# GpSimd in place of VectorE for 31 small softmax reciprocals, and later slots for work that waits on small DMAs

## The chip, the cores and the metric

The kernel runs on one core of a Trainium2 chip. The metric is the device time of one launch in microseconds (us), the median of several runs. Profiles are of one execution each; their span runs from the first to the last instruction, and times inside them count from the span's start.

## The reference

```
xn  = layernorm(x)                                    # x: 1 x 2048 x 512, bf16
q,k,v = split(xn @ wqkv)                              # 32 heads of 16
p   = softmax(q k^T * 16**-0.5)                       # 32 heads, 2048 x 2048 each
att = (p v, heads side by side) @ wo
g   = xn @ W_gate;  u = xn @ W_up                     # 512 -> 1792
out = x + att + (max(g, 0) * u) @ W_down
```

## The kernel before

One core does an attention block and a gated block of the same input. Queries are cut into four column blocks of 512 (`c4`), heads into four groups of eight (`gg`), each of which is done in two halves of four heads (`ee`). That makes 32 blocks `(c4, gg, ee)`, numbered n = 0 to 31. A block goes over 16 key tiles of 128 (`kt`), with four heads side by side: TensorE (PE) makes the scores (L1018), their exponential is taken, and a second matmul (L999) sums exponential times V in one PSUM bank, together with a row of sums of the exponentials.

The exponential is shared between two engines. ScalarE (ACT) does most tiles, in **score groups** of three or two tiles (`units` in the code, 663 of them): the scores of a group go to `ps_sc`, which has two slots, and one ACTIVATE (L1086) turns them into `ring`. 98 of the (block, kt) pairs go to VectorE (DVE) instead, and I call each of these a **D group**: four scores, one after the other through the single bank `ps_b[2]` (in the code `dsc`), are each read by a TENSOR_SCALAR (L1034), and four passes over 2048 columns follow: L1046, L1048, L1050 and, as the last, L1051. The results (`dring`) enter the same sum, with `v_aug` and `vd` as weights.

When a block's sum is complete, DVE copies it from PSUM to SBUF (L945; the copy lives in a part of `Wv`), and the normalisation follows as a chain of small steps: a DMA gathers the sums into `rsum` (L955), a reciprocal makes `rrec` (L956, on DVE), one DMA writes it to DRAM (`rec_scr`, L957), another spreads it over the partitions (`rb`, L960), and GpSimd (POOL) multiplies (L963). The result goes through DRAM once more (`o_scr`, L971 and L977, two blocks in one read) and is used as weights of the output projection with `Wo`, which closes the gated block's down projection in the same PSUM bank (`out_rows`). Block 31 is normalised on chip, without DMAs. The queries of each (c4, gg) are projected (`proj_q`), copied by DVE to `qT` (L670), written to DRAM (`q_scr`, L674) and read back as `qm` (L677). All DMAs are issued by SyncE (SP), in one queue.

Between the attention work stand the gated block's matmuls (`glu`: `wus` and `wgs`, then `Wd`), and matmuls with zeros as fillers that keep PE from being idle (L1116, L1123).

The order on each engine is decided when the program is built. `Graph.run` is a list scheduler: each operation has a priority, a duration and a latency that are written in the code, and the engine that can start first takes its best candidate. The engines then run these lists strictly in order, with semaphore waits. So a number in the source (a `lat=`, `D_LEAD`, a job's place) moves rows in the lists, and a wrong number makes an engine wait. `D_LEAD` says how many score groups ahead of its place a D group may start, `D_WAIT` adds to the priority number of its scores (higher is later), `PV_MIN` says from which score group on a second matmul may be placed, `RIDE` how long a score may be held to go beside others in TensorE's rows, and `job(upos(c4, gg) - 32, ...)` places the query projection that many score groups ahead of its block.

Of the kernel before, what the change touches and what calls it, by code (L numbers as in the profile page):

```python
# [16 lines left out]
DH = 16  # L17
# [12 lines left out]
PV_LAG = 4.0  # L30
PV_MIN = 3
NWS = 3
# [5 lines left out]
D_TAIL = 4  # L38
D_LEAD = 10.0
D_WAIT = 0.0  # L40

# [35 lines left out]
class Graph:  # L77
# [5 lines left out]
    KEEP = 4.0  # L83
    RIDE = 150.0
    WINDOW = 3400.0
# [311 lines left out]
def bass_parallel_sum__mha_block__glu_gated_reglu__prompt_kernel(  # L397
# [16 lines left out]
    with ExitStack() as es:  # L414
        def sb(name, shape, dt):
            return es.enter_context(nc.sbuf_tensor(name, shape, dt))
# [3 lines left out]
        hmask = sb("hmask", [128, 2], FP32)  # L420
        expo = sb("expo", [128, 4], FP32)
        warm = sb("warm", [128, 2], FP32)
        stats = sb("stats", [128, NT, 6], FP32)
# [69 lines left out]
             reads=[t_id], writes=[t_id], prio=-898)  # L493
        t_vones, t_woz = Tile(), Tile()
        G.op("POOL", 2500, lambda e: e.memset(v_aug[:, :, :, DH:VN], 1.0), writes=[t_vones], prio=-500)
# [159 lines left out]
        def proj_q(c4, gg, prio=0.0, tile=None, sub=0, eng="DVE", slots=None):  # L655
# [12 lines left out]
            else:  # L668
# [5 lines left out]
                dma(lambda e: e.dma_start(q_scr[par, :, 0:DH, :], qT[:, tr.slot, :]), 128,  # L674
                    reads=[tr] + t_qz, writes=[tqs], prio=prio - 60, stream=("qw", par), dur=500, lat=1400)
                for ee in range(2):
                    dma(lambda e, ee=ee: e.dma_start(qm[:, tq.slot, ee, :], q_pick(par, ee)), 128,  # L677
                        reads=[tqs], writes=[tq] if ee == 0 else [], prio=prio - 60 + 0.1 * ee, stream=("qr%d" % ee, par), dur=500, lat=1700)
                o = G.ops[-1]
# [200 lines left out]
        for c4 in range(NB):  # L880
            for gg in range(NGG):
                if (c4, gg) != (0, 0):
                    job(upos(c4, gg) - 32, 2, lambda s, c4=c4, gg=gg: proj_q(c4, gg, slots=s))
        for c4 in range(NB):
# [55 lines left out]
        def normalise(c4, gg, ee):  # L940
# [11 lines left out]
            if n >= 2:  # L952
                ts.r.extend(last_rec[n - 2][0].r)
                trr.r.extend(last_rec[n - 2][1].r)
            dma(lambda e: e.dma_start(rsum[:, par, :], o_sb[DH:128:32, to.slot, :]), 8, reads=[to], writes=[ts], prio=pr - 50, stream=("n1", n % 4), dur=600, lat=1600)  # L955
            G.op("DVE", 260, lambda e: e.reciprocal(rrec[:, par, :], rsum[:, par, :]), reads=[ts], writes=[trr], prio=-940)  # L956
            dma(lambda e: e.dma_start(rec_scr[n].rearrange("j (i q) -> (j i) q", q=16), rrec[:, par, :]), 8,  # L957
                reads=[trr], writes=[tsc], prio=pr - 50, stream=("n2", n % 4), dur=340, lat=1100)
            last_rec[n] = (ts, trr)
            dma(lambda e: e.dma_start(rb[:, trb.slot, :], rec_scr[n].unsqueeze(1).to_broadcast([4, 32, 512])), 256,  # L960
                reads=[tsc], writes=[trb], prio=pr - 50, stream=("n3", n % 4), dur=580, lat=4500)
            tn = Tile("oT", P_oT)
            G.op("POOL", 1280, lambda e: e.tensor_tensor(oT_of(tn), o_sb[:, to.slot, :], rb[:, trb.slot, :], ALU.mult),  # L963
                 reads=[to, trb], writes=[tn], prio=pr)
            if (c4, gg) == (NB - 1, NGG - 1):
# [5 lines left out]
            dma(lambda e: e.dma_start(o_scr[par, :, ee, :, :], oT_of(tn)), 128,  # L971
                reads=[tn], writes=[tos], prio=pr - 50, stream=("ow%d" % ee, par), dur=500, lat=1400)
            if ee:
                tw = t_oT[(c4, gg)] = Tile("oT", P_oT)
                t = o_scr[par, :, :, :, :]
                src = bass.AP(tensor=t.tensor, offset=t.offset, ap=[(32 * 512, 8), (512, DH), (1, 512)])
                dma(lambda e: e.dma_start(oT_of(tw), src), 128,  # L977
                    reads=[t_os[(c4, gg, 0)], tos], writes=[tw], prio=pr - 50, stream=("or", par), dur=500, lat=1800)
                o_last[par] = [G.ops[-1]]
# [179 lines left out]
```

## Time and profile before

| | |
|---|---|
| median of 3 runs | 848.86 us (847.76 to 857.77) |
| profiled execution: its own time | 849.45 us |
| profiled execution: span | 847.7 us, mean granted TensorE clock 0.971 |
| matmuls with zeros of L1116 | 624 |

The page of the profile has the busy time of each engine first; engines overlap, and PE, DVE and ACT are each busy for about nine tenths of the span. The groups by line then give a mean duration and the idle time of the engine just ahead of the group's instructions, with who ended it ("<-"). In a table of stretches, the figures after the comma are busy us and instructions of PE, PEld (weight loads), DVE, ACT and POOL, then the granted clock of TensorE, the DMA engines' share and GB/s.

### The profile page before, as it was taken

How to read it: one execution, taken by the hardware profiler on the slowest of the kernel's cores; microseconds unless marked ns; L12 is line 12 of the kernel's file. 1: busy time of each engine (PE TensorE's matmuls, PEld its weight loads, DVE VectorE, ACT ScalarE, POOL GpSimd, SP SyncE). 2: the span in 40 equal slices, each digit the busy share in tenths (PEclk: the TensorE clock that was granted, in tenths of full speed). 3: DMA queues.
4: the chain of work that ended last, by engine and by line, in shares of the span. 5: the costliest groups of instructions: out<-in, count | busy, mean ns of one | idle time of the engine just before them, and what ended most of it. 6: DMA issues, size and time to landing. Idle time of an engine off the chain costs nothing.

```text
span 847.7 us, 21183 instructions
## 1 busy us (share of the span) xinstructions
PE 785.1 (93%) x9378; PEld 227.3 (27%) x9378; DVE 759.2 (90%) x1101; ACT 765.6 (90%) x670; POOL 56.9 (7%) x58
## 2 busy tenths in 40 slices
PE   8979999899999999999899999989897998998996
PEld 3322222222222222222222222222222222222232
DVE  6969999899898899989898899999898898997984
ACT  5788999899799998989899999999987998997974
POOL 3100100000000000000000000100000000000100
PEclk9999999999799998999999999999999999999999
DMA  6024211211111121222101122221201112233001
GB/s 195 12 82 108 52 51 43 55 39 46 39 33 52 45 71 45 70 57 58 52 23 55 40 65 70 56 69 42 58 20 57 43 43 76 53 76 81 28 21 38
DMA packets 96131, 47.09 MB, mean 56 GB/s; under 512 B 70184, under 2 KB 92072, under 8 KB 96040
## 3 DMA queue, kind: packets, MB, share of 16 engines
q1 hardware_dynamic: 96040, 45.74, 20.0%
q8 instruction: 73, 1.20, 0.6%
q14 instruction: 18, 0.15, 0.1%
HBM read 36.96 MB, written 8.51 MB: 54 GB/s over the span
## 4 chain that ended last, share of the span: by engine, by line
DVE 50%; PE 34%; DMA 9%; ACT 4%; issue 1%; SPq 1%; POOL 0%; DVEq 0%; POOLq 0%
DVE dring L1034 16%; PE ps_b L643 14%; PE ps_sc L1018 9%; DVE dring L1050 8%; DVE dring L1051 8%; PE ps_b L999 7%; DVE dring L1046 4%; ACT ring L1086 4%; DVE dring L1048 4%; DMA rsum<-Wv 4%; DVE up_sb L812 3%; PE ps_b L1018 2%; DVE hT L816 2%; DVE Wv L945 1%; DMA q_scr<-qT 1%; DMA qm<-q_scr 1%
## 5 line engine op out<-in xcount | busy, mean ns | idle before, releaser
L1086 ACT ACTIVATE ring<-ps_sc 128x1536 bf16<-128x1536 f32 (+1 forms) x663 | 761.1, 1264 | 63.9 <-PE ps_sc L1018 32.5
L1034 DVE TENSOR_SCALAR dring<-ps_b 128x512 uint16<-128x512 f32 x392 | 267.8, 683 | 40.1 <-PE ps_b L1018 36.4
L1018 PE MATMUL ps_sc<-qm,kT 32*128 32x512 bf16 x1656 | 272.9, 392 | 3.8 <-ACT ring L1086 1.9
L1018 PE MATMUL ps_b<-qm,kT 32*128 32x512 bf16 x392 | 153.8, 392 | 24.0 <-DVE dring L1034 16.9
L999 PE MATMUL ps_b<-ring,v_aug 128*17 128x512 bf16 x1656 | 155.6, 389 | 2.4 <-DVE Wv L945 2.3
L1018 PEld LDWEIGHTS ps_sc<-qm,kT 32*128 32x128 bf16 x1656 | 63.5, 91 | 230.8 <-ACT ring L1086 171.5
L1051 DVE TENSOR_TENSOR dring<-dring 128x2048 bf16<-128x2048 bf16 x98 | 121.4, 1239 | 0.1
L1050 DVE TENSOR_TENSOR dring<-dring 128x2048 f16<-128x2048 bf16 x98 | 120.5, 1229 | 0.0
L963 POOL TENSOR_TENSOR x_sb<-Wv,rb 128x512 bf16<-128x512 f32 x26 | 38.4, 1479 | 608.8 <-DMA rb<-rec_scr 513.4
L643 PE MATMUL ps_b<-xnT,wgs 128*32 128x512 bf16 x896 | 67.0, 389 | 7.4 <-DVE up_sb L812 6.8
L643 PE MATMUL ps_b<-xnT,wus 128*32 128x512 bf16 x896 | 68.8, 401 | 5.1 <-DVE hT L816 5.1
L1046 DVE TENSOR_SCALAR dring<-dring 128x2048 uint16<-128x2048 uint16 x98 | 70.8, 722 | 1.5
L643 PE MATMUL ps_b<-Wd,hT 128*32 128x512 bf16 x896 | 67.5, 390 | 4.6 <-DMA x_sb<-o_scr 3.0
L1048 DVE TENSOR_SCALAR dring<-dring 128x2048 uint16<-128x2048 uint16 x98 | 71.3, 727 | 0.0
L999 PE MATMUL ps_b<-dring,vd 128*17 128x512 bf16 x784 | 69.5, 390 | 0.0
L1018 PEld LDWEIGHTS ps_b<-qm,kT 32*128 32x128 bf16 x392 | 35.7, 91 | 89.9 <-DVE dring L1034 61.7
L999 PEld LDWEIGHTS ps_b<-ring,v_aug 128*17 128x17 bf16 x1656 | 38.3, 89 | 73.9 <-issue 56.3
L1116 PE MATMUL ps_b<-zeros 128*17 128x512 bf16 x624 | 54.5, 397 | 0.0
L999 PE MATMUL ps_b<-dring,v_aug 128*17 128x512 bf16 x392 | 39.5, 393 | 4.0 <-DVE dring L1051 3.7
L812 DVE COPY up_sb<-ps_b 128x512 f32<-128x512 f32 x56 | 38.1, 681 | 1.6 <-PE ps_b L643 1.4
L816 DVE SCALAR_TENSOR_TENSOR hT<-ps_b,up_sb 128x512 bf16<-128x512 f32 x56 | 38.2, 682 | 0.8 <-PE ps_b L643 0.7
L643 PEld LDWEIGHTS ps_b<-xnT,wgs 128*32 128x32 bf16 x896 | 18.3, 95 | 37.4 <-DVE up_sb L812 17.0
(77 smaller groups left out, 333.4 us busy)
## 6 DMA issues: line engine op xcount, KB each, us to landing
rb<-rec_scr SPq DMA_DIRECT2D x31, 256.0 KB
wus<-in_B_W_up_dram SPq DMA_DIRECT2D x56, 128.0 KB, 2.9
wgs<-in_B_W_gate_dram SPq DMA_DIRECT2D x56, 128.0 KB, 2.3
qm<-q_scr SPq DMA_DIRECT2D x30, 128.0 KB
o_scr<-x_sb SPq DMA_DIRECT2D x25, 128.0 KB
q_scr<-qT SPq DMA_DIRECT2D x17, 128.0 KB
xr_sb<-in_A_x_dram SPq DMA_DIRECT2D x16, 128.0 KB, 2.6
out_dram<-xn_sb SPq DMA_DIRECT2D x16, 128.0 KB, 1.7
```

The costliest lines, as they stand in the source:

```text
L643: ins = e.matmul(bank_of(tile, sub)[32 * j:32 * j + 32, :], st[:, 32 * j:32 * j + 32], mv, start=(i == 0), stop=(i == n - 1), tile_positio ...
L812: G.op("DVE", 610, lambda e: e.tensor_copy(up_sb[:, tup.slot, :], bank_of(tu)), reads=[tu], writes=[tup], prio=slots[1])
L816: G.op("DVE", 610, lambda e: e.scalar_tensor_tensor(out=hT[:, FT * th.slot + ft, :], in0=bank_of(tg), scalar=0.0, in1=up_sb[:, tup.slot, : ...
L999: ins = e.matmul(ps_b[32 * j:32 * j + VN, 0, :], v, src[j][1](k), start=(first and k == 0), stop=(last and (k == 2 or not on)), tile_posit ...
L1018: return e.matmul(bank, kT[32 * j:32 * j + 32, gg, 128 * kt:128 * kt + 128], qm[32 * j:32 * j + 32, t_q[(c4, gg)].slot, ee, :], start=True ...
L1034: o = G.op("DVE", 610, lambda e, j=j: e.tensor_scalar(dring[:, tr.slot, 0, 512 * j:512 * j + 512].bitcast(U16), ps_b[:, 2, :], 0.25 * LOG2 ...
L1046: G.op("DVE", 600, lambda e: e.tensor_scalar(b(2, U16), b(0, U16), 0x7F, 0x3F80, op0=ALU.bitwise_and, op1=ALU.bitwise_or), reads=[tr], wri ...
L1048: G.op("DVE", 600, lambda e: e.tensor_scalar(b(1, U16), b(0, U16), 0xFF80, N_MANT, op0=ALU.bitwise_and, op1=ALU.bitwise_or), reads=[tr], w ...
L1050: G.op("DVE", 1140, lambda e: e.tensor_tensor(b(2, FP16), b(2), b(2), ALU.mult), reads=[tm], writes=[tm], prio=u - 3, name="d4")
L1051: G.op("DVE", 1140, lambda e: e.tensor_tensor(b(2), b(0), b(2, FP16), ALU.mult), reads=[tm, tr], writes=[tm], prio=u - 3, name="d5")
L1086: return e.activation(ring[:, a:a + n, :], ps_sc[:, 3 * k0:3 * k0 + n, :], ACTF.Exp, scale=0.25)
L1116: ins = e.matmul(ps_b[32 * j:32 * j + VN, 0, :], zeros[:, 0:VN], zmov, start=False, stop=False, tile_position=(0, 32 * j))
```

## The change

The reciprocal of a block's sums leaves DVE's list and becomes a power of -1 on GpSimd, an elementwise TENSOR_TENSOR with the constant tile `minus`, whose operands and result are the same 128x16 floats; block 31 keeps its reciprocal on DVE. In the planner's numbers the small DMAs of the normalisation and of the queries get longer latencies, the query projection is placed 36 instead of 32 score groups ahead, D groups start at most 8 instead of 10 score groups ahead and their scores rank one later, second matmuls may follow two groups sooner, and a score is held for at most 100 instead of 150 ns. No operand, buffer or amount of arithmetic changes but for this.

```diff
-PV_MIN = 3
+PV_MIN = 1
...
-D_LEAD = 10.0
-D_WAIT = 0.0
+D_LEAD = 8.0
+D_WAIT = 1.0
...
-    RIDE = 150.0
+    RIDE = 100.0
...
+        minus = sb("minus", [128, 1], FP32)
...
-        t_vones, t_woz = Tile(), Tile()
+        t_vones, t_woz, t_minus = Tile(), Tile(), Tile()
+        G.op("POOL", 200, lambda e: e.memset(minus[:], -1.0), writes=[t_minus], prio=-400)
...
-                    reads=[tr] + t_qz, writes=[tqs], prio=prio - 60, stream=("qw", par), dur=500, lat=1400)
+                    reads=[tr] + t_qz, writes=[tqs], prio=prio - 60, stream=("qw", par), dur=500, lat=2400)
...
-                        reads=[tqs], writes=[tq] if ee == 0 else [], prio=prio - 60 + 0.1 * ee, stream=("qr%d" % ee, par), dur=500, lat=1700)
+                        reads=[tqs], writes=[tq] if ee == 0 else [], prio=prio - 60 + 0.1 * ee, stream=("qr%d" % ee, par), dur=500, lat=2700)
...
-                    job(upos(c4, gg) - 32, 2, lambda s, c4=c4, gg=gg: proj_q(c4, gg, slots=s))
+                    job(upos(c4, gg) - 36, 2, lambda s, c4=c4, gg=gg: proj_q(c4, gg, slots=s))
...
-            dma(lambda e: e.dma_start(rsum[:, par, :], o_sb[DH:128:32, to.slot, :]), 8, reads=[to], writes=[ts], prio=pr - 50, stream=("n1", n % 4), dur=600, lat=1600)
-            G.op("DVE", 260, lambda e: e.reciprocal(rrec[:, par, :], rsum[:, par, :]), reads=[ts], writes=[trr], prio=-940)
+            dma(lambda e: e.dma_start(rsum[:, par, :], o_sb[DH:128:32, to.slot, :]), 8, reads=[to], writes=[ts], prio=pr - 50, stream=("n1", n % 4), dur=600, lat=2600)
+            G.op("POOL", 3000, lambda e: e.tensor_tensor(rrec[:, par, :], rsum[:, par, :], minus[:, 0:1].to_broadcast([128, 16]), ALU.pow),
+                 reads=[ts, t_minus], writes=[trr], prio=pr - 50)
...
-                reads=[trr], writes=[tsc], prio=pr - 50, stream=("n2", n % 4), dur=340, lat=1100)
+                reads=[trr], writes=[tsc], prio=pr - 50, stream=("n2", n % 4), dur=340, lat=1600)
...
-                reads=[tsc], writes=[trb], prio=pr - 50, stream=("n3", n % 4), dur=580, lat=4500)
+                reads=[tsc], writes=[trb], prio=pr - 50, stream=("n3", n % 4), dur=580, lat=5300)
...
-                reads=[tn], writes=[tos], prio=pr - 50, stream=("ow%d" % ee, par), dur=500, lat=1400)
+                reads=[tn], writes=[tos], prio=pr - 50, stream=("ow%d" % ee, par), dur=500, lat=2400)
...
-                    reads=[t_os[(c4, gg, 0)], tos], writes=[tw], prio=pr - 50, stream=("or", par), dur=500, lat=1800)
+                    reads=[t_os[(c4, gg, 0)], tos], writes=[tw], prio=pr - 50, stream=("or", par), dur=500, lat=2600)
```

What this does to the lists is seen at three places. In DVE's list, at the end of block 14, the copy of the block's sum (the rows that write `Wv`) and what follows it stood like this before:

```order
L945 COPY Wv<-ps_b 128x512
L1034 TENSOR_SCALAR dring<-ps_b 128x512
L812 COPY up_sb<-ps_b 128x512
L1050 TENSOR_TENSOR dring<-dring 128x2048
L1034 TENSOR_SCALAR dring<-ps_b 128x512
L956 RECIPROCAL rrec<-rsum 128x16
L816 SCALAR_TENSOR_TENSOR hT<-ps_b,up_sb 128x512
L1034 TENSOR_SCALAR dring<-ps_b 128x512
L1051 TENSOR_TENSOR dring<-dring 128x2048
```

and stand like this now (line numbers are two or three higher after the change):

```order
L947 COPY Wv<-ps_b 128x512
L1037 TENSOR_SCALAR dring<-ps_b 128x512
L1054 TENSOR_TENSOR dring<-dring 128x2048
L1037 TENSOR_SCALAR dring<-ps_b 128x512
L814 COPY up_sb<-ps_b 128x512
L1049 TENSOR_SCALAR dring<-dring 128x2048
L1037 TENSOR_SCALAR dring<-ps_b 128x512
L1053 TENSOR_TENSOR dring<-dring 128x2048
L818 SCALAR_TENSOR_TENSOR hT<-ps_b,up_sb 128x512
```

The reciprocal, which waited for the DMA into `rsum`, is gone from between the score reads, and with it all 31 such rows of this list; nothing in DVE's list waits for a DMA of the normalisation any more.

In GpSimd's list, after its last start-up row (`Wo_p`), before:

```order
L504 MEMSET Wo_p 128x1024
L963 TENSOR_TENSOR oT<-Wv,rb 128x512
L963 TENSOR_TENSOR x_sb<-Wv,rb 128x512
L500 MEMSET ident 128x128
L501 AFFINE_SELECT ident<-ident 128x128
L963 TENSOR_TENSOR x_sb<-Wv,rb 128x512 x4
```

and now:

```order
L506 MEMSET Wo_p 128x1024
L958 TENSOR_TENSOR rrec<-rsum,minus 128x16
L966 TENSOR_TENSOR oT<-Wv,rb 128x512
L958 TENSOR_TENSOR rrec<-rsum,minus 128x16
L502 MEMSET ident 128x128
L503 AFFINE_SELECT ident<-ident 128x128
L966 TENSOR_TENSOR x_sb<-Wv,rb 128x512
```

Each multiplication by `rb` now has its power ahead of it, and so it goes on to block 30: power and multiplication of one block, then those of the next.

In PE's list, around the projection of the queries (`Wq`) of the last head group (`c4` = 3, `gg` = 3), before:

```order
L999 MATMUL ps_b<-dring,vd 17x512 x8
L1018 MATMUL ps_b<-qm,kT 128x512
L643 MATMUL ps_b<-xnT,Wq 32x512 x4
L1018 MATMUL ps_sc<-qm,kT 128x512 x3
L643 MATMUL ps_b<-xnT,Wq 32x512 x4
L1018 MATMUL ps_sc<-qm,kT 128x512 x2
L643 MATMUL ps_b<-xnT,Wq 32x512 x8
L999 MATMUL ps_b<-ring,v_aug 17x512 x4
L1018 MATMUL ps_b<-qm,kT 128x512
```

and now:

```order
L1002 MATMUL ps_b<-dring,vd 17x512 x4
L1021 MATMUL ps_sc<-qm,kT 128x512 x2
L645 MATMUL ps_b<-xnT,Wq 32x512 x16
L1002 MATMUL ps_b<-dring,vd 17x512 x4
L1021 MATMUL ps_sc<-qm,kT 128x512 x3
L1021 MATMUL ps_b<-qm,kT 128x512
L1002 MATMUL ps_b<-ring,v_aug 17x512 x4
```

From the last of the `Wq` rows to the first score of this head group there stood 6 score groups before, and there stand 14 now. Counted in the same way in PE's list, the smallest such distance of all query projections goes from 6 to 13 (the next smallest before were 8 and 10). The distance from the last second matmul of block 23 to the first matmul that needs its normalised result goes from 14 to 21 score groups (block 7: 14 to 20, block 15: 15 to 20, block 30: 9 to 14). The distance from the fourth score of a D group to the first second matmul that uses it falls: its median over the 98 groups goes from 10 to 7 score groups, and the groups at 6 or less go from 3 to 35. The matmuls with zeros of L1116 go from 624 to 700. All other rows keep their number.

## The prediction

> **What bounds the kernel now.** I began with the head of the profile's page: what each engine is busy with, and for how long.
>
> ```profile
> span 847.7 us, 21183 instructions
> ## 1 busy us (share of the span) xinstructions
> PE 785.1 (93%) x9378; PEld 227.3 (27%) x9378; DVE 759.2 (90%) x1101; ACT 765.6 (90%) x670; POOL 56.9 (7%) x58
> ```
>
> Three engines at nine tenths: no single one explains the span, and a few us taken from one of them need not shorten it. So I looked for an engine whose idle time is lost for good. That is ACT, from its group of exponentials:
>
> ```profile
> L1086 ACT ACTIVATE ring<-ps_sc 128x1536 bf16<-128x1536 f32 (+1 forms) x663 | 761.1, 1264 | 63.9 <-PE ps_sc L1018 32.5
> ```
>
> 663 exponentials, one per score group, are 761.1 us of work (1.15 us each) which the change doesn't touch, and ACT sat idle for only 63.9 us ahead of them. The rest of the span is start and tail. What the change can bring has to come out of these 63.9 us, so I asked for stretches. First eleven in which some engine waited for a small DMA; the quoted rows are the last three of them and the sum of all:
>
> ```profile
> 216.00:229.00 13.00, 11.56 (x97) 2.46 (x93) 9.70 (x13) 9.02 (x8) 1.27 (x1) 0.70 0.14 43
> 776.00:781.00 5.00, 3.77 (x31) 0.86 (x31) 2.29 (x4) 0.94 (x1) 0.00 (x0) 0.66 0.29 81
> 645.00:655.00 10.00, 7.01 (x71) 1.79 (x74) 7.09 (x10) 5.84 (x5) 0.00 (x0) 0.83 0.21 66
> sum 88.00, PE 69.93 PEld 16.73 DVE 67.33 ACT 53.27 POOL 4.09; mean PE 6.36 PEld 1.52 DVE 6.12 ACT 4.84 POOL 0.37
> ```
>
> In 88.0 us ACT worked 53.3: 34.7 us lost, over half of all its idle time, in a tenth of the span. The clock (the figure after the busy times) is 0.66 to 0.83 here: it falls when PE has stood still, and PE's slow return lengthens the pause. Then eleven stretches between them, from 75:150 to 784:815, 582 us in all:
>
> ```profile
> sum 582.00, PE 560.47 PEld 161.19 DVE 560.49 ACT 572.64 POOL 35.91; mean PE 50.95 PEld 14.65 DVE 50.95 ACT 52.06 POOL 3.26
> ```
>
> There ACT is busy for 98.4% and DVE for 96.3%. Undisturbed, the kernel runs at ACT's pace, with DVE close behind it. A score group takes 1.148 / 0.984 = 1.17 us there.
>
> How a pause comes about is seen around 417 us, in order of time:
>
> ```profile
> 417.16 0.25 DVE L956 RECIPROCAL rrec<-rsum 128x16 f32<-128x16 f32 x1 [2.97 <-DMA rsum<-Wv]
> ...
> 418.01 0.61 PE L643 MATMUL ps_b<-xnT,wus 128*32 128x512 bf16 x8 [2.59 <-DVE hT L816]
> ...
> 418.99 1.02 ACT L1086 ACTIVATE ring<-ps_sc 128x1024 bf16<-128x1024 f32 x1 [2.08 <-PE ps_b L1018]
> ```
>
> DVE stood 2.97 us at a reciprocal of 0.25 us whose sums had not landed; PE stood behind DVE, ACT behind PE. Eight of the eleven stretches are of this kind. In two (216, 776) PE waited for `qm`, in one (645) for the normalised result, `x_sb` from `o_scr`. By the rows above these three cost ACT 4.0, 4.1 and 4.2 us, so the eight cost 34.7 - 12.3 = 22.4.
>
> **The change part by part.** *The reciprocals* leave DVE:
>
> ```profile
> L956 DVE RECIPROCAL rrec<-rsum 128x16 f32<-128x16 f32 x31 | 7.7, 248 | 19.0 <-DMA rsum<-Wv 18.8
> ```
>
> DVE gets back 31 x 248 ns = 7.7 us of work and 18.8 us of waiting. I don't add these to ACT's 22.4 us: it is the same loss, seen one engine further on. On GpSimd the 128x16 power isn't in the trace, but smaller ones are (layer norm):
>
> ```profile
> L574 POOL TENSOR_TENSOR rstd<-vare,expo 128x4 f32<-128x4 f32 x3 | 3.1, 1042 | 0.2
> L574 POOL TENSOR_TENSOR rstd<-vare,expo 128x1 f32<-128x1 f32 x4 | 2.3, 582 | 0.2
> ```
>
> One column 582 ns, four 1042: 153 ns a column, so 16 give 582 + 15 x 153 = 2.9 us (an estimate; bounds 1.0, as for four columns, and 9.3, sixteen times one). 31 of them are 90 us on an engine that is busy for 7% of the span, one per block, that is every 847.7 / 32 = 26 us. Queued behind a power are the multiplication of its own block, which needs it anyway, and on SP, behind the issue of `rec_scr` that waits for it, mostly `rb` and weight loads. So its price is that of a longer chain: 2.9 instead of 0.25 us before the normalised result (at 9.3 us the pause at 645 would be back, 4.2 us).
>
> *The chains and their new distances.* The normalisation of block 23, which ended late, and the queries of the last head group, in the chain that ended last:
>
> ```profile
> 635.24 1.63 DMA rec_scr<-rrec
> 636.88 5.07 DMA rb<-rec_scr
> 642.08 1.28 POOL x_sb L963
> 643.38 3.26 DMA o_scr<-x_sb
> 646.66 4.29 DMA x_sb<-o_scr
> 650.99 2.20 PE ps_b L643 x20
> ...
> 768.19 2.87 DMA q_scr<-qT
> 771.67 5.51 DMA qm<-q_scr
> 777.64 1.40 PE ps_b L643 x12
> ```
>
> From the issue of `rec_scr` to the landing it is 15.7 us. The whole chain, from the block's last matmul, outlasted its 14 score groups (16.3 us) by the pause, 4.2 us: some 20.5 us. The power adds 2.7: 23.2 us, where 21 groups are now 24.5. The wait ends, with 1.3 us to spare; blocks 7 and 15, which didn't wait at 14 and 15 groups, have more. Queries took 9.0 us from the issue to the landing; the copy ahead of them some 0.6 more; 6 groups are 7.0 us, 8 are 9.3, and both waited. The new smallest distance, 13, is 15.2 us. Even if SP holds `q_scr` for one power, 12.5 us fit. So I take all eleven pauses as gone: these 53.3 us of exponentials then take 53.3 / 0.984 = 54.1, which gains **88.0 - 54.1 = 33.9 us**. The spells of low clock go with them. Bounds: 22 (the reciprocals' alone) to 34.7.
>
> *Later D groups* (`D_LEAD`, `D_WAIT`, `PV_MIN`, `RIDE`) take cover away. PE needs the last product of a D group (L1051) 7 score groups after its fourth score instead of 10, and 35 of 98 groups stand at 6 or fewer instead of 3. The waits of before show the kind:
>
> ```profile
> PE ps_b L999 <- DVE dring L1051: 3.7, 4, 1.6
> ```
>
> Four waits of 0.93 us. Should every one of the 32 additional tight groups wait so, that is 30 us, the upper bound; the lower is 0, as most groups at 6 to 8 didn't wait before. As DVE is 96% busy it will often be late: I take half of them, 15 us on PE, and of this not quite half on ACT, which has two score slots in hand: **+6.5 us**.
>
> *Start and tail.* In PE's list the first query projection (16 matmuls) now stands ahead of the scores of the thirteenth group, where ACT already waits; and the four additions of the last rows (L868) stand between the steps of block 31's normalisation, no longer ahead of its copy.
>
> ```profile
> L643 PE MATMUL ps_b<-xnT,Wq 128*32 128x512 bf16 x240 | 18.4, 384 | 0.4 <-DVE xn_sb L855 0.3
> ...
> L868 DVE TENSOR_TENSOR xnT<-ps_b,xnT 128x512 f32<-128x512 f32 x4 | 2.8, 692 | 4.9 <-PE ps_b L643 4.9
> ```
>
> 18.4 / 15 = 1.2 us for the first, one of 15 such projections; three additions of 0.69 us for the second: together **+3.3 us** (bounds 0 and 5). The 76 more matmuls with zeros stand where PE would idle: 0, or, were PE short of time, 76 x 18.4 / 240 = 5.8 us by the same row. Other edits only set such places.
>
> Sum: 847.7 - 33.9 + 6.5 + 3.3 = 823.6 us of span. The profiled execution took 849.45 us, 1.75 more than its span and 0.6 more than the median of 848.86; I forecast **825 us**, 2.8% under the median. Measurements of this kernel tell a change from none at about 2%, here 832 and 866 us.
>
> **The rivals.** *D groups become the pause.* If PE waits at nearly all tight groups and ACT loses it in full, 30 us come back: 825 + 23.5 = 849, and half of that gives 837. For it: DVE is nearly full in the undisturbed stretches. Against: a wait under 1 us fits into ACT's slots.
>
> *The power holds up VectorE*, the case that ends slower. GpSimd and DVE already block each other:
>
> ```profile
> 35.28 1.04 POOL L574 TENSOR_TENSOR rstd<-vare,expo 128x4 f32<-128x4 f32 x1
> ...
> 35.98 0.30 DVE L703 TENSOR_SCALAR vd<-v_aug 128x544 bf16<-128x544 bf16 x1
> ...
> 423.60 1.27 POOL L963 TENSOR_TENSOR x_sb<-Wv,rb 128x512 bf16<-128x512 f32 x1 [24.89 <-DMA rb<-rec_scr]
> ...
> 423.86 2.10 DVE L1050 TENSOR_TENSOR dring<-dring 128x2048 f16<-128x2048 bf16 x1
> ...
> L1050 DVE TENSOR_TENSOR dring<-dring 128x2048 f16<-128x2048 bf16 x98 | 120.5, 1229 | 0.0
> ```
>
> The DVE pass L1050, 1.23 us in the mean, took 2.10 when it started during a multiplication, and ended 1.09 us after it, as if it had only started then. The pass at 35.98 started inside a power and ended (36.28) before it (36.32). If the 2.9 us power blocks like a multiplication, one of the passes L1046 to L1051 runs into nearly each of the 31, and stands for some 2 us (2.9 less 0.9 until one comes): 60 us on DVE. The eight waits turned 18.8 us of DVE into 22.4 of ACT, so up to 72; with half of it hidden 36. That is 825 + 36 to 72, or 861 to 897; I take 880. It decides from 41 us lost, 1.3 us a power. The row at 35.98 speaks against it; it is one row of a shorter power.
>
> The Trainium skill, "SBUF — State Buffer", section "Who interferes with whom", says that GpSimd and VectorE share a pair of ports under an exclusive lock which is held for the whole instruction, and that VectorE operations with two SBUF inputs or in a two-port mode fall under it. By that rule the change ends in this rival. The multiplication's row agrees with it, the power's row doesn't.
>
> *The waits stay, one engine on.* If SP, which now waits for a power ahead of other DMAs, makes weights or queries late, the three other pauses stay (12.3 us) and the weights' come on top, say as much again: 825 + 12 to 25, about 843.
>
> **How the numbers follow.** Forecast, 811 to 836: 0.62. D groups, 836 to 850: 0.20. Waits that stay, 837 to 850: 0.09. The power's lock, 861 to 897: 0.09. Low end: 847.7 - 34.7 with nothing given back, and a few us less where other short waits go too, 811. High end 848: it leaves out the lock and the top of the two middle cases. Faster by over 2% is most of the forecast, 0.55; slower is the lock, 0.09; the rest, 0.36.
>
> **What would show it.** ACT's idle time ahead of L1086 falls from 63.9 to about 40 us, and the granted clock rises above 0.971. No wait of DVE for `rsum`; POOL's new group at about 2.9 us; waits of PE for `qm` or `x_sb` under 1 us. PE's wait for L1051 rises to some 15 us. Were L1050 and its sisters longer in the mean (L1050 is at 1229 ns), it is the lock. I'd be wrong on size, above all, where tight D groups pass their waits on in full.

## The result, and the profile after

The changed kernel takes **815.51 us** (median of 4 runs, 813.30 to 820.19), beside 851.18 us for the kernel before in the same session: a ratio of 0.9579, 95% interval 0.9502 to 0.9657. In a later session it took 816.30 us, ratio 0.9644 (0.9573 to 0.9715). The time is 9.5 us under the forecast of 825 us. The profiled execution took 813.30 us, 1.8 more than its span, as before. Of the two runs of the kernel with the power alone, below, the second profile is read, since the first fell in a disturbed execution, at a granted clock of 0.960.

The head of the page of the changed kernel, and from its groups the exponentials, the powers and VectorE's last pass of a D group:

```profile
span 811.5 us, 21329 instructions
## 1 busy us (share of the span) xinstructions
PE 768.7 (95%) x9450; PEld 227.5 (28%) x9450; DVE 757.1 (93%) x1070; ACT 763.2 (94%) x670; POOL 156.1 (19%) x90
```

```profile
L1089 ACT ACTIVATE ring<-ps_sc 128x1536 bf16<-128x1536 f32 (+1 forms) x663 | 758.6, 1257 | 30.6 <-PE ps_sc L1021 19.4
L958 POOL TENSOR_TENSOR rrec<-rsum,minus 128x16 f32<-128x16 f32 x31 | 98.0, 3162 | 370.8 <-DMA rsum<-Wv 370.8
L1054 DVE TENSOR_TENSOR dring<-dring 128x2048 bf16<-128x2048 bf16 x98 | 123.0, 1255 | 0.1
```

The span is 36.2 us shorter. ACT's idle time ahead of the exponentials fell by 33.3 of these (63.9 to 30.6), the exponentials themselves by 2.5 (761.1 to 758.6), and 0.4 are start and tail. So nearly all of the gain is idle time of ACT. GpSimd, on the other hand, now waits 370.8 us for the very sums for which DVE waited 18.8. Nothing urgent stands behind it: SP waits for the powers (74.8 us in 23 places), but no wait of PE, DVE or ACT is put down to one.

Three stretches show the pace (us; busy time of PE, PEld, DVE, ACT, POOL; then the clock). Between the first two lies the one pause for a DMA that is left:

```profile
43.00:245.00 202.00, 192.28 (x2325) 54.81 (x2317) 193.77 (x269) 199.06 (x175) 39.30 (x18) 1.00 0.22 58
250.00:766.00 516.00, 496.74 (x6087) 143.92 (x6091) 493.68 (x672) 506.74 (x443) 96.91 (x42) 1.00 0.21 56
766.00:801.00 35.00, 33.37 (x463) 10.67 (x451) 27.04 (x36) 28.87 (x26) 5.61 (x3) 1.00 0.09 27
```

In the first two ACT is busy for 98.5% and 98.2%: the pace that only the undisturbed stretches had before (98.4%) now holds for 718 of the 811.5 us, at full clock. Near the end it doesn't: ACT loses 6.4 us in three waits (2.27 at 767.15, 2.93 at 773.36, 1.21 at 792.75), where before it lost 4.18 in one; but for 1.14 us at 797.46, PE works there without a wait of 0.9 us or more, on long runs of other matmuls between the scores. Spells at half clock, worked out from the mean clock, came to 49.7 us before and are down to 5.5. The pause, in order of time (rows of SP, in whose list the transfers are issued, and of the engines that wait):

```profile
232.89 0.59 SPq L676 DMA_DIRECT2D q_scr<-qT  x1
...
233.13 1.27 POOL L966 TENSOR_TENSOR x_sb<-Wv,rb 128x512 bf16<-128x512 f32 x1 [6.63 <-DMA rb<-rec_scr]
...
235.74 1.10 SPq L679 DMA_DIRECT2D qm<-q_scr  x2
236.89 0.55 SPq L974 DMA_DIRECT2D o_scr<-x_sb  x1
237.48 0.48 SPq L850 DMA_DIRECT2D xr_sb<-in_A_x_dram  x1
243.34 0.60 SPq L980 DMA_DIRECT2D x_sb<-o_scr  x1
...
246.40 2.32 PE L645 MATMUL ps_b<-Wd,hT 128*32 128x512 bf16 x20 [2.23 <-DMA x_sb<-o_scr]
...
249.31 2.36 ACT L1089 ACTIVATE ring<-ps_sc 128x1536 bf16<-128x1536 f32 x2 [3.57 <-PE ps_sc L1021]
```

It is block 7's normalised result. The multiplication ended at 234.40, but SP stood at the read of `qm`, which waits for `q_scr`, and issued `o_scr` only at 236.89. That write took 6.43 us, with the two reads of `qm` issued just ahead of it and a read of `x` behind it; 3.26 us was its time in the chain before (at 643.38, where the two reads of `qm` came 1.13 us after it). What slowed it is not shown. PE waited 2.23 us, ran the next 3 us at half clock (first row below; the second is the stretch behind it), and ACT lost 3.57:

```profile
246.40:249.40 3.00, 3.00 (x27) 0.85 (x31) 0.15 (x1) 0.09 (x1) 2.62 (x1) 0.50 0.00 0
249.40:255.00 5.60, 5.60 (x76) 1.59 (x68) 2.88 (x5) 5.58 (x5) 0.27 (x1) 0.98 0.03 4
```

### The profile page after: what moved, and what is told of

It reads as the page before. It is cut to its first block, busy times and chain, and to the rows that moved or that the text cites. A ratio compares the mean times of both kernels' runs of the same rounds, so it can differ in the third digit from the quotient of the medians.

```text
span 811.5 us, 21329 instructions
## 1 busy us (share of the span) xinstructions
PE 768.7 (95%) x9450; PEld 227.5 (28%) x9450; DVE 757.1 (93%) x1070; ACT 763.2 (94%) x670; POOL 156.1 (19%) x90
## 3 DMA queue, kind: packets, MB, share of 16 engines
q8 instruction: 74, 1.21, 0.6%
## 4 chain that ended last, share of the span: by engine, by line
DVE 60%; PE 35%; DMA 2%; ACT 1%; issue 1%; SPq 0%; DVEq 0%
DVE dring L1037 19%; PE ps_b L645 13%; DVE dring L1053 10%; PE ps_sc L1021 9%; DVE dring L1054 9%; PE ps_b L1002 8%; DVE dring L1049 6%; DVE dring L1051 5%; PE ps_b L1021 3%; DVE hT L818 3%; DVE up_sb L814 3%; DVE Wv L947 2%; ACT ring L1089 1%; PE ps_b L1119 1%; DVE kT L692 1%; DMA o_scr<-x_sb 1%
## 5 line engine op out<-in xcount | busy, mean ns | idle before, releaser
L1089 ACT ACTIVATE ring<-ps_sc 128x1536 bf16<-128x1536 f32 (+1 forms) x663 | 758.6, 1257 | 30.6 <-PE ps_sc L1021 19.4
L1021 PE MATMUL ps_sc<-qm,kT 32*128 32x512 bf16 x1656 | 266.7, 385 | 4.6 <-ACT ring L1089 2.6
L958 POOL TENSOR_TENSOR rrec<-rsum,minus 128x16 f32<-128x16 f32 x31 | 98.0, 3162 | 370.8 <-DMA rsum<-Wv 370.8
L1021 PE MATMUL ps_b<-qm,kT 32*128 32x512 bf16 x392 | 150.4, 384 | 14.2 <-DVE dring L1037 11.5
L1002 PE MATMUL ps_b<-ring,v_aug 128*17 128x512 bf16 x1656 | 141.0, 381 | 4.2 <-DVE Wv L947 4.0
L1002 PE MATMUL ps_b<-dring,vd 128*17 128x512 bf16 x784 | 67.6, 381 | 0.0
L645 PE MATMUL ps_b<-Wd,hT 128*32 128x512 bf16 x896 | 64.9, 389 | 2.3 <-DMA x_sb<-o_scr 2.2
L645 PE MATMUL ps_b<-xnT,wus 128*32 128x512 bf16 x896 | 65.7, 383 | 0.9 <-DVE hT L818 0.7
L1119 PE MATMUL ps_b<-zeros 128*17 128x512 bf16 x700 | 58.1, 382 | 0.0
L1002 PEld LDWEIGHTS ps_b<-ring,v_aug 128*17 128x17 bf16 x1656 | 36.4, 89 | 65.7 <-issue 39.6
```

Of the source, the lines that this page charges most:

```text
L645: ins = e.matmul(bank_of(tile, sub)[32 * j:32 * j + 32, :], st[:, 32 * j:32 * j + 32], mv, start=(i == 0), stop=(i == n - 1), tile_positio ...
L958: G.op("POOL", 3000, lambda e: e.tensor_tensor(rrec[:, par, :], rsum[:, par, :], minus[:, 0:1].to_broadcast([128, 16]), ALU.pow), reads=[t ...
L1002: ins = e.matmul(ps_b[32 * j:32 * j + VN, 0, :], v, src[j][1](k), start=(first and k == 0), stop=(last and (k == 2 or not on)), tile_posit ...
L1021: return e.matmul(bank, kT[32 * j:32 * j + 32, gg, 128 * kt:128 * kt + 128], qm[32 * j:32 * j + 32, t_q[(c4, gg)].slot, ee, :], start=True ...
L1089: return e.activation(ring[:, a:a + n, :], ps_sc[:, 3 * k0:3 * k0 + n, :], ACTF.Exp, scale=0.25)
L1119: ins = e.matmul(ps_b[32 * j:32 * j + VN, 0, :], zeros[:, 0:VN], zmov, start=False, stop=False, tile_position=(0, 32 * j))
```

## The experiments

**Each half of the change alone.** First the power on GpSimd, with every number of the planner as before (run twice):

```diff
...
-            G.op("DVE", 260, lambda e: e.reciprocal(rrec[:, par, :], rsum[:, par, :]), reads=[ts], writes=[trr], prio=-940)
+            G.op("POOL", 3000, lambda e: e.tensor_tensor(rrec[:, par, :], rsum[:, par, :], minus[:, 0:1].to_broadcast([128, 16]), ALU.pow),
+                 reads=[ts, t_minus], writes=[trr], prio=pr - 50)
```

> The kernel before, with only the reciprocal moved to GpSimd as a power; all latencies, query slots and D group settings as before. Theory 'waits' (the gain is ACT's pauses behind waits for small DMAs, and nothing else): the eight pauses at the reciprocal go, 22 us; the waits for qm stay (two query projections stand 5 and 9 score groups ahead of their use in this order) and so does one for x_sb, and each costs ACT about 4 us: 851 - 22 + 0 to 4 = 829 to 833 us. Theory 'slots' (what counts are the planner's later slots and the D group settings, and the reciprocal's engine is of no account): 845 to 855 us. Theory 'lock' (the power holds up DVE): DVE's passes over 2048 columns get longer in the mean by over 0.2 us, and the time is 850 us or more.

> The kernel before with the power on GpSimd alone, again, for a profile at an undisturbed clock: the earlier one measured 840 us where the waits gave 829 to 833. 'The planner, which counts 3.0 us for a power, put other work at smaller distances': the same waits of TensorE again, for qm near 775 us (4.7 us) and x_sb near 251 (2.6), the one near the start 1.6 us longer, and 833 to 841 us. 'The earlier profile was only of a disturbed run': those waits gone and 829 to 833.

Measured: 840.24 us (ratio 0.9879, 0.9799 to 0.9959), then 839.81 us (0.9887, 0.9805 to 0.9968). Beside the first, the kernel before took 845.93. I had expected 829 to 833, so that was a miss. From the second profile, in order of time, the largest wait:

```profile
765.57 0.61 PE L1021 MATMUL ps_sc<-qm,kT 32*128 32x512 bf16 x3 [4.92 <-DMA qm<-q_scr]
766.22 2.37 ACT L1089 ACTIVATE ring<-ps_sc 128x1536 bf16<-128x1536 f32 x2 [6.57 <-PE ps_b L1021]
```

No wait of DVE for `rsum` is left. But the planner has made another list around its longer operation, and in it the last queries are projected 5 score groups ahead of their use. There ACT loses 6.57 us, and at 249.54 another 5.07 to the normalised result of block 7, whose chain is 2.65 us longer now. This is the case "the planner put other work at smaller distances", and the 833 to 841 us given for it fit; ACT's idle time is 50.1 us, 13.8 less than before.

Then the other half, all the planner's numbers as after the change, with the reciprocal on DVE:

```diff
-            G.op("POOL", 3000, lambda e: e.tensor_tensor(rrec[:, par, :], rsum[:, par, :], minus[:, 0:1].to_broadcast([128, 16]), ALU.pow),
-                 reads=[ts, t_minus], writes=[trr], prio=pr - 50)
+            G.op("DVE", 260, lambda e: e.reciprocal(rrec[:, par, :], rsum[:, par, :]), reads=[ts], writes=[trr], prio=-940)
```

> The changed kernel with the reciprocal back in VectorE's list, and everything else as changed. Theory 'waits': the longer latency of the gather (2600 instead of 1600) puts the reciprocal later in DVE's list, so most of the eight waits for rsum should go here too, with 2 to 8 us of DVE's 18.8 left; one query projection stands 4 score groups ahead of its use and costs ACT 4 to 6 us: 820 to 832 us. Theory 'engine' (a reciprocal in DVE's list waits wherever it stands): DVE waits 12 us or more for rsum, 835 to 842 us.

Measured: 832.67 us (0.9817, 0.9745 to 0.9890), at the upper edge of the 820 to 832 of "waits". Its waits (us in total, times, longest):

```profile
DVE rrec L958 <- DMA rsum<-Wv: 7.0, 6, 1.8
...
PE ps_b L645 <- DMA oT<-o_scr: 3.1, 1, 3.1
PE ps_b L645 <- DMA x_sb<-o_scr: 2.7, 2, 2.0
```

The later slots cut DVE's waiting for sums from 18.8 to 7.0 us, but don't end it. ACT's largest pause is at the last queries again, 6.43 us at 761.17: they stand 4 score groups ahead of their use in this list, the reads of `qm` were issued at 754.62, and from 752.71 to 760.74 PE has no score to do. So the halves bring 1.2% and 1.8%, each under the 2% that these measurements tell from none, and together 4.2%. The planner makes a list of its own for each: with either half alone the last queries stand 4 or 5 groups ahead, with both 14.

**The waits alone.** In the kernel before, with its lists as they were, the reciprocal is taken of a constant and so waits for nothing. The normalisation by the sums is thereby left out.

```diff
...
-            G.op("DVE", 260, lambda e: e.reciprocal(rrec[:, par, :], rsum[:, par, :]), reads=[ts], writes=[trr], prio=-940)
+            G.op("DVE", 260, lambda e, p2=par: e.reciprocal(rrec[:, p2, :], ones16[:]), reads=[ts], writes=[trr], prio=-940, name="rec")
+            no_wait.append((G.ops[-1], list(ts.w)))
...
+        for o, ws in no_wait:
+            for w in ws:
+                o.deps.pop(w, None)
```

> The kernel before with the same order on every engine, but each of the 31 reciprocals is taken of a constant tile and no longer waits for the gathered sums (so the normalisation is left out of the result); its 248 ns on DVE, all DMAs and all other waits stay. Theory 'waits': DVE's 18.8 us of waiting for rsum are gone and ACT gets back the 22.4 us of the eight pauses: 851 - 22 = 829 us (825 to 834), granted clock 0.983 or more; the pauses at qm and x_sb (12 us on ACT) stay. Rival 'saturated' (DVE and PE are so full that a pause taken away comes back at the next place): 840 to 850 us.

Measured: 821.58 us (0.9699, 0.9634 to 0.9764), 24.4 us under the kernel before in that session. That is below the 825 to 834 that I expected, mostly since I had counted from 851 us and the kernel before took 845.93 there. Groups and waits:

```profile
L1090 ACT ACTIVATE ring<-ps_sc 128x1536 bf16<-128x1536 f32 (+1 forms) x663 | 758.7, 1269 | 38.6 <-PE ps_sc L1022 17.2 <-PE ps_b L1022 14.3 <-PE ps_b L1003 5.0
...
L959 DVE RECIPROCAL rrec<-ones 128x16 f32<-128x16 f32 x31 | 7.6, 244 | 0.0
```

```profile
PE ps_b L1022 <- DMA qm<-q_scr: 4.8, 2, 3.2
...
PE ps_b L645 <- DMA x_sb<-o_scr: 4.0, 1, 4.0
```

ACT's idle time fell by 25.3 us while DVE does the same work in the same places; what remains are the pauses for `qm` and `x_sb`, as the prediction's split had it, and the one near the end. So the eight waits for `rsum` cost about 25 us, and they are shown to be the larger part of the gain.

**The old numbers for D groups**, in the changed kernel:

```diff
-PV_MIN = 1
+PV_MIN = 3
...
-D_LEAD = 8.0
-D_WAIT = 1.0
+D_LEAD = 10.0
+D_WAIT = 0.0
...
-    RIDE = 100.0
+    RIDE = 150.0
```

> The changed kernel with PV_MIN 3, D_LEAD 10, D_WAIT 0 and RIDE 150 as before: the reciprocals on GpSimd, the latencies and the query slots stay changed. Theory 'waits': the D group settings are of little account; 811 to 824 us, as the changed kernel (815.5) with up to two waits for qm more (two query projections stand 9 score groups ahead of their use here, not 13), 4 us each. Theory 'D groups pay' (the settings, which I had put at a cost of 6.5 us, bring a part of the gain): 828 us or more. My prediction's term read strictly, a cost of 6.5 us for the settings: 809 us.

Measured: 815.59 us (0.9626, 0.9556 to 0.9695), within the noise of the changed kernel's 815.51 (0.9579) of the session before. Its waits and its exponentials:

```profile
PE ps_b L1002 <- DVE dring L1054: 0.9, 4, 0.3
```

```profile
L1089 ACT ACTIVATE ring<-ps_sc 128x1536 bf16<-128x1536 f32 (+1 forms) x663 | 757.3, 1268 | 33.5 <-PE ps_sc L1021 14.3 <-PE ps_b L1002 10.8 <-PE ps_b L1021 6.5
```

The row for the first in the changed kernel:

```profile
PE ps_b L1002 <- DVE dring L1054: 4.7, 14, 1.1
```

With the old numbers PE waits 3.8 us less for the last product of a D group, and ACT doesn't gain: it is idle for 33.5 us, 2.9 more than in the changed kernel. This list has no pause at block 7, but loses 3.13, 2.61 and 2.40 us in three waits near the end. So these numbers, with the lists that the planner makes from them, are of no account for the time; what they alone would do with all other rows in place is not shown.

**Does a power hold VectorE up?** Two kernels, both with 23 more operations on GpSimd ahead of the powers of blocks 8 to 30, and with the lists of DVE, ACT and GpSimd else unchanged. One has a second power of the same sums, the other a multiplication of a constant over 1160 columns, written over the tile `Wk` once its last reader is done; nobody reads either.

```diff
+        jrec = sb("jrec", [128, 16], FP32)
...
-            G.op("POOL", 3000, lambda e: e.tensor_tensor(rrec[:, par, :], rsum[:, par, :], minus[:, 0:1].to_broadcast([128, 16]), ALU.pow),
+            G.op("POOL", 3000, lambda e: (n >= 8 and e.tensor_tensor(jrec[:], rsum[:, par, :], minus[:, 0:1].to_broadcast([128, 16]), ALU.pow), e.tensor_tensor(rrec[:, par, :], rsum[:, par, :], minus[:, 0:1].to_broadcast([128, 16]), ALU.pow))[1],
```

```diff
-            G.op("POOL", 3000, lambda e: e.tensor_tensor(rrec[:, par, :], rsum[:, par, :], minus[:, 0:1].to_broadcast([128, 16]), ALU.pow),
+            G.op("POOL", 3000, lambda e: (n >= 8 and e.tensor_tensor(Wk[:, :, 0:290], minus[:, 0:1].unsqueeze(1).to_broadcast([128, 4, 290]), minus[:, 0:1].unsqueeze(1).to_broadcast([128, 4, 290]), ALU.mult), e.tensor_tensor(rrec[:, par, :], rsum[:, par, :], minus[:, 0:1].to_broadcast([128, 16]), ALU.pow))[1],
...
+            if n >= 8:
+                for t in t_wk:
+                    for r in t.r:
+                        G.ops[-1].deps[r] = True
```

> The changed kernel, with a second power of the same size and the same sums ahead of the power of each block from the ninth on: 23 more, about 2.9 us each, nothing else moved. 'A power does not hold VectorE up': VectorE's passes keep their means (L1053 1.24 us, L1054 1.26 in the changed kernel), and only the two longer chains can wait: the normalised results of blocks 15 and 23, 20 and 21 score groups ahead of their use, up to 3 us each. 815.5 + 0 to 6 us, 818. 'The port is locked for the whole power': some 2 us on VectorE for each, 23 x 2.0 = 46 us, half of it or all on ScalarE, 839 to 862 us.

> The same place and about the same length of GpSimd time as in the run with two powers (1160 columns; by the 128x512 multiplication at 1.27 us, 2.9 us), but spent on a multiplication of a constant that nobody reads, from the ninth block on. 'A streaming operation holds VectorE up, a power does not': one of VectorE's two-input or fast passes stands for some 2 us at most of the 23, up to 46 us on VectorE, and ScalarE, which VectorE follows at 96%, loses half to all of it: 839 to 862 us, 845, with L1051 to L1054 longer in their means. 'What GpSimd does is of no account, only the chain's length': as with two powers, 818 us.

Measured: with two powers 822.55 us (0.9711, 0.9646 to 0.9776), with the multiplication **850.26 us** (1.0029, 0.9979 to 1.0079): the whole gain is gone. The changed kernel beside them took 816.30. Groups with two powers:

```profile
L1055 DVE TENSOR_TENSOR dring<-dring 128x2048 bf16<-128x2048 bf16 x98 | 123.5, 1261 | 0.1
...
L959 POOL TENSOR_TENSOR jrec<-rsum,minus 128x16 f32<-128x16 f32 x23 | 73.0, 3175 | 233.2 <-DMA rsum<-Wv 233.2
```

and with the multiplication, then one of its places in order of time:

```profile
L1093 ACT ACTIVATE ring<-ps_sc 128x1536 bf16<-128x1536 f32 (+1 forms) x663 | 763.6, 1254 | 59.0 <-PE ps_sc L1025 39.7 <-PE ps_b L1025 9.2 <-PE ps_b L1006 7.8
...
L1058 DVE TENSOR_TENSOR dring<-dring 128x2048 bf16<-128x2048 bf16 x98 | 132.1, 1348 | 0.1
...
L958 POOL TENSOR_TENSOR Wk<-minus 128x1160 bf16<-128x1160 f32 x23 | 55.6, 2417 | 261.1 <-DMA rsum<-Wv 261.1
```

```profile
760.55 2.12 POOL L958 TENSOR_TENSOR Wk<-minus 128x1160 bf16<-128x1160 f32 x1 [10.47 <-DMA rsum<-Wv]
760.73 3.02 DVE L1058 TENSOR_TENSOR dring<-dring 128x2048 bf16<-128x2048 bf16 x1
762.63 3.87 POOL L958 TENSOR_TENSOR rrec<-rsum,minus 128x16 f32<-128x16 f32 x1
```

The multiplication is shorter than a power (2.12 us undisturbed, 2.4 in the mean) and yet holds DVE: the pass that starts 0.18 us after it takes 3.02 us instead of 1.22, and ends 1.08 after it. 18 of the 23 lengthen a pass over 2048 columns so, by 23.0 us together, and ACT's idle time rises from 30 to 59. The power in the last row starts as the multiplication ends, and now it is the power that waits (3.87 us instead of 2.90), while the pass goes on. The 23 extra powers lengthen none. The 6.25 us by which that kernel is slower than the changed one are about the top of the 0 to 6 that I gave its longer chains: PE waits 2.14 us at 635.06 for the result of block 23. The two extra operations differ in kind and in size (16 columns against 1160), so which of these decides is not told apart. DVE's reads of PSUM over 512 columns that start during the multiplication keep their 0.68 to 0.69 us. The multiplications by `rb`, over 512 columns, hold DVE up too, and did before: 23 passes are lengthened by 14.1 us together in the changed kernel, 16 by 11.3 before.

**More distance.** The changed kernel with two DMAs estimated 2.0 and 1.8 us longer, and other places:

```diff
-                    job(upos(c4, gg) - 36, 2, lambda s, c4=c4, gg=gg: proj_q(c4, gg, slots=s))
+                    job(upos(c4, gg) - 38, 2, lambda s, c4=c4, gg=gg: proj_q(c4, gg, slots=s))
...
-                    job(upos(c4 + 1) + 10 + 12 * i, 9, lambda s, c4=c4, i=i: out_rows(c4, i, range(4), True, True, slots=s), 2)
+                    job(upos(c4 + 1) + 14 + 12 * i, 9, lambda s, c4=c4, i=i: out_rows(c4, i, range(4), True, True, slots=s), 2)
...
-                    job(upos(c4 + 1) - 54 + 10 * i, 8, lambda s, c4=c4, i=i: out_rows(c4, i, range(2), True, False, slots=s), 2)
+                    job(upos(c4 + 1) - 40 + 8 * i, 8, lambda s, c4=c4, i=i: out_rows(c4, i, range(2), True, False, slots=s), 2)
...
-                reads=[tn], writes=[tos], prio=pr - 50, stream=("ow%d" % ee, par), dur=500, lat=2400)
+                reads=[tn], writes=[tos], prio=pr - 50, stream=("ow%d" % ee, par), dur=500, lat=4400)
...
-                    reads=[t_os[(c4, gg, 0)], tos], writes=[tw], prio=pr - 50, stream=("or", par), dur=500, lat=2600)
+                    reads=[t_os[(c4, gg, 0)], tos], writes=[tw], prio=pr - 50, stream=("or", par), dur=500, lat=4400)
```

> The changed kernel with 2 us more of estimated latency for each of the two DMAs of the normalised result, queries projected two score groups earlier, and the rows of the output 4 groups later (those of the last block's first half 14 groups later, 8 instead of 10 apart). Blocks 7, 15 and 23 then stand 23 to 25 groups ahead of their use (20, 20 and 21 before), the smallest distance of a query is 17 instead of 13. 'Each pause is a chain against its distance': the pause of 3.6 us at block 7 goes, and 1 to 3 us of the 6.4 us that ScalarE waits near the end with it: 815.5 - 3.6 - 2 = 810 us (808 to 813). 'What is left is set by other things' (the tail, the clock): 815 to 818.

> The changed kernel itself again, beside the other three on the same chip. Every theory: 815.5 us, 813 to 820, and the one pause at block 7 in the profile again.

> The kernel with more distance itself again, in more rounds, beside the other two: 809.7 us, 808 to 812, with no wait of TensorE over 0.9 us after the start. If its lead over the changed kernel was only that of a few lucky runs: 813 to 816.

Measured: **809.72 us** (0.9568, 0.9512 to 0.9624; runs from 809.07 to 812.01), beside 816.30 us for the changed kernel (812.27 to 821.41), and in the next session 809.20 us (0.9539, 0.9480 to 0.9598; 806.66 to 812.06). It beats both kernels, the changed one by 0.8% of the medians in the session that they shared, where its slowest run (812.01) is under the changed kernel's fastest (812.27). The changed kernel, run again, has the pause at block 7 again (3.36 us of ACT). Its exponentials:

```profile
L1089 ACT ACTIVATE ring<-ps_sc 128x1536 bf16<-128x1536 f32 (+1 forms) x663 | 758.6, 1265 | 25.7 <-PE ps_sc L1021 13.5 <-PE ps_b L1021 6.1 <-PE ps_b L1002 4.3
```

No wait of PE for a DMA of these chains is left, and ACT's idle time fell by 4.9 us. In the repeated run PE waits 0.94 us at 601.92 and 1.03 at 720.05, both for DVE, where I had expected none over 0.9. Of the remaining 25.7, 5.30 are one wait at the start, where PE does the projections.

**Is GpSimd needed?** The kernel with more distance, with the reciprocals on DVE again. The planner counts 5.0 us of latency for their sums there; with the power it counts 2.6, and before the change it counted 1.6 (the bracket in the expectation has these figures muddled).

```diff
-... dur=600, lat=2600)
-            G.op("POOL", 3000, lambda e: e.tensor_tensor(rrec[:, par, :], rsum[:, par, :], minus[:, 0:1].to_broadcast([128, 16]), ALU.pow),
-                 reads=[ts, t_minus], writes=[trr], prio=pr - 50)
+... dur=600, lat=5000)
+            G.op("DVE", 260, lambda e: e.reciprocal(rrec[:, par, :], rsum[:, par, :]), reads=[ts], writes=[trr], prio=-940)
```

> The kernel with more distance, but with the reciprocals on VectorE again, each planned 5.0 us behind the issue of its sums' DMA (0.8 us more than the planner's 1.6 + 0.6 in the kernel before would be 2.2; so 2.8 us later than there). 'What cost was the wait at the head of VectorE's queue, not the work or its engine': no wait of VectorE for rsum over 0.5 us, 7.7 us of work back on VectorE of which little reaches ScalarE, no powers: as with more distance, 808 to 814 us, 811. 'GpSimd is needed' (VectorE is full, and whatever it gets back ScalarE loses, or the sums still land late here and there): 817 to 825 us.

Measured: 823.71 us (0.9670, 0.9595 to 0.9744). Two of its six runs took 813.57 and 814.92 us, at a granted clock of 0.995 and 0.992, and four 822.00 to 826.20, at 0.974 to 0.984; the profile is of one of the four. Its rows:

```profile
L958 DVE RECIPROCAL rrec<-rsum 128x16 f32<-128x16 f32 x31 | 7.7, 247 | 0.0
```

```profile
L1088 ACT ACTIVATE ring<-ps_sc 128x1536 bf16<-128x1536 f32 (+1 forms) x663 | 759.4, 1270 | 35.5 <-PE ps_sc L1020 20.1 <-PE ps_b L1020 7.4 <-PE ps_b L1001 6.2
```

No reciprocal waits any more, and still ACT idles 9.8 us longer than with the power. Either the 7.7 us of work count, or the lists, which the planner made anew. The last kernel tells these apart: the kernel with more distance, with 32 reciprocals of a constant added on DVE, one ahead of each block's copy (31 in the expectation), and every other row of DVE, ACT and GpSimd in its place.

```diff
...
-            G.op("DVE", 610, lambda e: e.tensor_copy(o_sb[:, to.slot, :], ps_b[:, 0, :]), reads=[tp], writes=[to], prio=-950, name="oev%d" % n)
+            G.op("DVE", 610, lambda e: (e.reciprocal(jrec[:], ones16[:]), e.tensor_copy(o_sb[:, to.slot, :], ps_b[:, 0, :]))[1], reads=[tp], writes=[to], prio=-950, name="oev%d" % n)
```

> The kernel with more distance, with 31 reciprocals of a constant added on VectorE, each right ahead of a block's copy; they wait for nothing that the copy doesn't wait for, nobody reads them, and every other row keeps its place. So VectorE has the 7.7 us of work again that it had before the change, and none of the waiting. 'The work itself counts little, the waits were all': 809 to 811 us. 'VectorE is full, so its work comes back on ScalarE': up to 7.7 us, 813 to 817. If the run with late reciprocals on VectorE (823.7 us) was slow for its work and not for its changed lists, this one should come near it, 817 or more.

Measured: 810.87 us (0.9535, 0.9487 to 0.9583), where the same lists without these rows took 809.20 and 809.72 in the other sessions.

```profile
L1092 ACT ACTIVATE ring<-ps_sc 128x1536 bf16<-128x1536 f32 (+1 forms) x663 | 760.5, 1258 | 28.6 <-PE ps_sc L1024 15.8 <-PE ps_b L1024 5.8 <-PE ps_b L1005 4.3
...
L950 DVE RECIPROCAL jrec<-ones 128x16 f32<-128x16 f32 x32 | 7.8, 244 | 0.1
```

The work itself costs little, as 809 to 811 us was to show: 1 to 2 us by these medians, which are of different sessions, and nothing by the ratios (0.9535 beside 0.9539 and 0.9568). So, by exclusion, the late reciprocals were slow for their lists. Which rows of those lists did it stays open: in that kernel the longest waits of PE after the start are 1.06 us at 316, 1.07 at 510 and 1.47 at 683, each for DVE, and its spells at half clock come to 25.4 us, against 15.9 in the repeated run with more distance. A list that has the reciprocals on DVE and is as fast is not ruled out.

## Why the prediction was right, point by point

- **ACT's idle time is what can be won, and the eleven pauses hold most of it: right.** Predicted gain 33.9 us by their going; ACT's idle time fell by 33.3. That the two are so close is in part luck: ACT still lost 3.57 us at block 7 and 2.2 more than before near the end, and short waits outside the eleven pauses, on which I had not counted, fell by some 4.4. The split into 22.4 for the sums and 12.3 for `qm` and `x_sb` holds too: without the waits for sums alone, ACT gained 25.3 and the rest stayed.
- **"All eleven gone": one wasn't.** Of blocks 7 and 15 I had said that they "have more" to spare, as they didn't wait before. For block 7 the step failed: a chain's DMAs don't take the same time everywhere, and `o_scr` took 6.43 us instead of the 3.26 that I had from block 23, after a start 2.5 us late behind `qm` on SP. It is like the third rival, "the waits stay, one engine on", at one place, 3.57 us; but what SP stood at was the read of the queries, not a power. In the kernel with more distance, three groups more, it is gone.
- **Later D groups, +6.5 us: the term that was mis-sized.** PE's wait for the last product rose to 4.7 us in 14 waits, not to 15, and none of it reached ACT beyond what the old numbers lose as well (815.59 against 815.51 us). The reason that I gave against the first rival, a wait under 1 us fits into ACT's slots, I should have applied to the term itself: 14 waits of 0.34 us in the mean left ACT little to lose.
- **Start and tail, +3.3 us: 0.4 the other way.** The wait at the start is 5.30 us in both profiles, so the projection ahead of it found room; from ACT's last exponential to the end it is 10.4 us where it was 10.9, so no cost of the additions among block 31's steps shows.
- These two terms make 9.8 us; with them at 0 the sum is 847.7 - 33.9 = 813.8 of span, and the profile has 811.5. Of the other 2.3 us, the exponentials' own 2.5 are not explained; I had taken them as untouched.
- **The power's price: right.** Estimate 2.9 us; undisturbed it takes 2896 ns (the median; 3162 in the mean).
- **The lock, the rival on the other side: refuted for the power, and true for a multiplication.** In the changed kernel, 51 of DVE's passes over 2048 columns start during a power, and the longest takes 1.22 us. One such place in order of time:

```profile
56.24 2.90 POOL L958 TENSOR_TENSOR rrec<-rsum,minus 128x16 f32<-128x16 f32 x1 [20.11 <-DMA rsum<-Wv]
56.43 1.22 DVE L1054 TENSOR_TENSOR dring<-dring 128x2048 bf16<-128x2048 bf16 x1
...
58.16 0.68 DVE L1051 TENSOR_SCALAR dring<-dring 128x2048 uint16<-128x2048 uint16 x1
```

The Trainium skill, "SBUF — State Buffer", section "Who interferes with whom", gives the shared ports to whichever of the two engines starts first, for its whole instruction. The run with the multiplication agrees (18 of 23, 23.0 us), and so does a power that starts during a DVE pass over 2048 columns: the power is lengthened (4.03 us at 102.28). A pass that starts during a power isn't lengthened, and there the measurement decides. The row at 35.98 in the profile of before, one short power, had it right. Its price was of the right order: 23 multiplications cost 28 us against the kernel with two powers and 34 against the changed one, 1.2 to 1.5 us each, where the rival would have decided from 1.3.

- **What would show it:** the clock rose (0.971 to 0.997), no wait of DVE for `rsum` was left, and ACT's idle time came down to 30.6 rather than 40, since the 9.8 us of the two terms were not lost. Of the waits for `qm` and `x_sb`, one of 2.23 us was over the 1 us that I gave.

## What to carry to other kernels

An instruction of a quarter of a microsecond can cost over ten times its length where it waits for a small DMA at the head of a queue that runs in order, on an engine for which others wait: here eight waits cost some 25 us, and the work of the reciprocals without a wait 1 to 2 by the medians. One way out is to move such a wait to an engine with nothing urgent behind it, even if the work takes twelve times as long there, and to give all that hangs on the chain as much more distance; alone these brought 1.2% and 1.8% of the 4.2%. When GpSimd is that engine, look at what it runs: a power of 16 columns beside VectorE was free, a multiplication of 1160 columns, shorter in time, gave the whole gain back.

## What the runs showed of the hardware

- A GpSimd power of 128x16 takes 2896 ns, 582 for one column and 1042 for four: some 154 ns a column. It doesn't hold up VectorE's passes with two SBUF inputs or between SBUF tiles (51 started during one, none took over 1.22 us), but it is held up itself when it starts during one (4.03 us here):

```profile
102.05 1.22 DVE L1054 TENSOR_TENSOR dring<-dring 128x2048 bf16<-128x2048 bf16 x1
102.28 4.03 POOL L958 TENSOR_TENSOR rrec<-rsum,minus 128x16 f32<-128x16 f32 x1 [8.96 <-DMA rsum<-Wv]
```

- In the two profiles of the changed kernel and the two with extra work on GpSimd, each of the seven waits of PE of 1.9 us or more after the start came with 3.4 or 6.8 us at half clock, which began within the wait or at most 1.4 us after its end; of those from 1.1 to 1.7 us only some did. At 246.40 a wait of 2.23 us went with 3.57 lost by ACT. Such waits are not the only cause: the two profiles with more distance have five such spells ahead of their last one, and no wait of PE over 1.1 us after the start.
- The write of 128 KB to `o_scr` took 3.26 us in one place and 6.43 in another, where two reads had been issued just ahead of it: a distance that is enough for a chain in one place isn't for the same chain elsewhere.
